# Weight decode at one chunk per double step, feed-forward of the first batch thinned and then packed, transposed copies on ScalarE

## The chip, the core and the metric

The kernel runs on one core of one Trainium2 chip. A core has five engines with instruction queues of their own: PE (TensorE, matrix products and transposes into PSUM), DVE (VectorE), ACT (ScalarE), POOL (GpSimd) and SP (SyncE, which issues DMAs). Each engine executes its queue in order and waits where a semaphore is not yet there. The metric is the device time of one execution in microseconds, as the median of several runs. A profiled execution gives besides this a trace with the start and the end of every instruction.

## The reference, cut to what matters

```python
# q, k, v: (4, 8, 768, 64); centroids: (8, 16, 64); w_in: (512, 2048); w_out: (2048, 512)
q_assign = argmax(q_n . c_n)          # nearest of 16 centroids, per head
k_assign = argmax(k_n . c_n)
mask   = q_assign[..., :, None] == k_assign[..., None, :]
scores = where(mask, q @ k.T / 8, -1e9)
attn   = softmax(scores) @ v          # per batch and head, 768 x 768 scores
x = attn.transpose(0, 2, 1, 3).reshape(3072, 512)
h = x @ w_in
out = (h * clip(h + 3, 0, 6) / 6) @ w_out
```

The weights come to the kernel as 64-bit floats; they are read as pairs of 32-bit words and turned into 32-bit floats in the kernel ("decoded"). The other inputs are 32-bit floats.

## The kernel before

**Units of work.** The 32 heads are treated as 16 pairs; four pairs make a batch of 768 tokens. Each pair has 12 steps (two halves of the queries, six blocks of 128 keys), so there are 192 steps, numbered n. The main loop (line 527) takes two steps at a time. Such a turn of the loop is called a double step here; r is n modulo 12 and tells its place within the pair. The order in which instructions are issued is written out by hand (`tc.manual_schedule()`), and every engine keeps to it.

**One double step**, in the order of issue: `scores` for two steps (PE products into `ps`, line 346, ACT exponential `ex`, line 358, POOL running sum `acc`, lines 362 and 365), `attn_v` for two steps (PE `pv`, line 375), the checks `in_range` of an earlier division on ACT (lines 409 and 411), at r = 2 and r = 8 a `divide` (PE `pd`, line 396, DVE reciprocal `rcp`, line 400, DVE product into `xT`, line 401), then feed-forward items and preparation items of the next pair in turns, and at the end the weight chunks that fall due.

**Preparation of the next pair** (`prep_items`, line 470): at r = 0 and r = 2 two parts each of `turn` (PE transposes of q and k into a PSUM tile `pqk`, line 278, then a copy of it into `xf`: on DVE, line 283, for the even parts, on ACT, line 281, for the odd ones); at r = 4 `route` (PE `pr`, line 292, and a chain of DVE operations, lines 298 to 314, that ends in `one_hot`); at r = 8 and r = 10 `route_turn` (PE `po`, line 326, and ACT copy `xm`, line 330).

**PSUM scratch.** `pqk`, `pr`, `po` and `pd` all come from `scratch` (line 165). As long as `st["early"]` holds, two of three come from the two buffers of `psum_m`; from n = READY = 52 on, all come from the single buffer of `psum_t`, and `psum_m` serves the feed-forward (`ph`, `py`). From then on a scratch tile can be written only after the reader of the one before it has finished.

**Feed-forward items** (`ffn_items`, line 419): for each half of a batch's tokens 16 `up` items (8 matmul instructions into `ph`, line 426, ACT `t`, line 433, DVE `gT`, line 435) and 12 `down` items (8 matmul instructions into `py`, line 448; each fourth ends in a DVE copy `y` and an output DMA). A batch has 56 items, 32 of them `up`. How many items are issued by step n is set by `items_by`.

**Weight decode** (`decode_weights`, line 202): 32 chunks of 128 x 512, 16 of w_in, then 16 of w_out. Each is loaded by one DMA into `raw` (two buffers, line 200), summed up by two ACT operations (`wsize`, lines 208 and 211) and decoded by five DVE operations (`wtop` and `wunit`, lines 217, 221, 224 and 228, and the result, line 231). How many chunks are issued by step n is set by `chunks_by`. The `down` items of the first batch need all of w_out, so they cannot come before DECODED.

Of the kernel before, what the change touches and what calls it, by code (L numbers as in the profile page):

```python
# [19 lines left out]
NCH = S // P  # L20
# [10 lines left out]
NW = NKT * DFF // WC + NFT  # L31
# [85 lines left out]
def fast_path(ctx, tc, ok, q, k, v, centroids, moe_w_in, moe_w_out, out):  # L117


    nc = tc.nc  # L120
# [44 lines left out]
    def scratch(shape, name):  # L165

        st["scratch"] += 1
        if st["early"] and st["scratch"] % 3:
            return psum_m.tile(shape, F32, name=name, tag="m")
        return psum_t.tile(shape, F32, name=name, tag="t")  # L170
# [100 lines left out]
    def turn(g, part):  # L271
        if part == 0:
            st["xf", g] = xp.tile([P, NC2, P], F32, name="xf")
        qk, xf = st["qk", g], st["xf", g]
        pt = scratch([P, NHC, P], "pqk")
        for i in range(NHC):
            j = part * NHC + i
            nc.tensor.transpose(out=pt[:, i], in_=qk[:, j // NCH, j % NCH], identity=ident)  # L278
        dst = xf[:, part * NHC : (part + 1) * NHC]
        if part % 2:  # L280
            nc.scalar.copy(out=dst, in_=pt)  # L281
        else:
            nc.vector.tensor_copy(out=dst, in_=pt)  # L283
        if part == 3:
            st.pop(("qk", g))

# [183 lines left out]
    def prep_items(g, r):  # L470

        if g >= NPAIR:
            return []
        if r in (0, 2):
            return [lambda: turn(g, r), lambda: turn(g, r + 1)]
        return {
            4: [lambda: route(g)],
            8: [lambda: route_turn(g, 0), lambda: route_turn(g, 1)],
            10: [lambda: route_turn(g, 2)],
        }.get(r, [])  # L480

    per_pair = 2 * NCH
    per_batch = NKT * per_pair
    total = NPAIR * per_pair
    lag_v, lag_d = 2, 4
    up_half = NFT
    per_ffn = 2 * (NFT + NHC * 4)


    DECODED, READY = 5 * per_batch // 3, per_batch + lag_d  # L490

    def chunks_by(n):
        if n <= per_batch:
            return n // 5
        first = per_batch // 5
        return min(first + (n - per_batch) * (NW - first) // (DECODED - 2 - per_batch), NW)

    def items_by(n):

        if n <= DECODED:  # L500
            return max(n - READY, 0) * up_half // (DECODED - READY)
        if n <= READY + per_batch:
            rest = per_ffn - up_half
            return up_half + (n - DECODED) * rest // (READY + per_batch - DECODED)
        return per_ffn + (n - READY - per_batch) * per_ffn // per_batch

    st["early"] = True
    fill, later = [], []
# [2 lines left out]
    with tc.manual_schedule():  # L511
# [6 lines left out]
        for part in range(4):  # L518
            turn(0, part)
# [7 lines left out]
        for n in range(0, total + lag_d + 2, 2):  # L527
# [17 lines left out]
            if r == 6:  # L545
                load(g + 2, "q", "k")
                load(g + 1, "v")
            prep = prep_items(g + 1, r)
            want = items_by(n + 2) - done if n < total else len(fill)
            want = min(want, len(fill))  # L550
            done += want
# [5 lines left out]
            for i in range(chunks_by(n), chunks_by(n + 2)):  # L557
                load_weights(i + 1)
                decode_weights(i)
# [9 lines left out]
    for got, sums, high in ((good, totals, BOUND), (fit, w_totals, W_HIGH)):  # L569
        for a, bound in enumerate((high, 0.0)):  # L570
            nc.vector.tensor_scalar(
                out=got[:, a], in0=sums[:, a], scalar1=bound, scalar2=None, op0=ALU.is_le
# [320 lines left out]
@with_exitstack  # L893
def kernel(
    ctx: ExitStack,
    tc: tile.TileContext,
    q: bass.AP,
    k: bass.AP,
    v: bass.AP,
    centroids: bass.AP,  # L900
    moe_w_in: bass.AP,
    moe_w_out: bass.AP,
    out: bass.AP,
):
    ins = (q, k, v, centroids, moe_w_in, moe_w_out)
    flagp = ctx.enter_context(tc.tile_pool(name="flagp", bufs=1))
    ok = flagp.tile([1, 1], I32, name="ok")
    with ExitStack() as inner:
        fast_path(inner, tc, ok, *ins, out)
    with tc.If(tc.nc.values_load(ok[0:1, 0:1], min_val=0, max_val=1) == 0):  # L910
        with ExitStack() as inner:
            general_path(inner, tc, *ins, out)
# [32 lines left out]
```

The two planning functions give, before the change: 9 chunks up to n = 48, then 23 in the 15 double steps up to n = 78, one or two in each. Items of the first batch: 16 `up` items between n = 52 and n = 80, then the other 40 items in the 10 double steps up to n = 100, four in each. After that 56 items in 48 steps.

## Time and profile before

| What | Value |
|---|---|
| Median of 5 runs | 1167.17 us (1163.58 to 1171.08) |
| Profiled execution, its own time | 1162.99 us |
| Span of its trace | 1160.9 us |
| Mean granted TensorE clock | 0.979 |
| PE busy | 1106.0 us, 95% of the span |
| DVE busy | 396.9 us, 34% |
| ACT busy | 364.4 us, 31% |
| POOL busy | 299.9 us, 26% |

The profile's page gives busy time per engine over the whole span, then the same in 40 equal slices, then a chain of waits that led to the end and the costliest groups of instructions. The prediction reads the slices first, then sums over chosen stretches of time, and then single waits. Idle time of PE is the time to look for, since PE is the engine that is busy nearly to the end; idle time of another engine costs nothing by itself.

### The profile page before, as it was taken

How to read it: one execution, taken by the hardware profiler on the slowest of the kernel's cores; microseconds unless marked ns; L12 is line 12 of the kernel's file. 1: busy time of each engine (PE TensorE's matmuls, PEld its weight loads, DVE VectorE, ACT ScalarE, POOL GpSimd, SP SyncE). 2: the span in 40 equal slices, each digit the busy share in tenths (PEclk: the TensorE clock that was granted, in tenths of full speed). 3: DMA queues.
4: the chain of work that ended last, by engine and by line, in shares of the span. 5: the costliest groups of instructions: out<-in, count | busy, mean ns of one | idle time of the engine just before them, and what ended most of it. 6: DMA issues, size and time to landing. Idle time of an engine off the chain costs nothing.

```text
span 1160.9 us, 11468 instructions
## 1 busy us (share of the span) xinstructions
PE 1106.0 (95%) x4610; PEld 554.6 (48%) x4610; DVE 396.9 (34%) x531; ACT 364.4 (31%) x692; POOL 299.9 (26%) x187
## 2 busy tenths in 40 slices
PE   6998968879999999999999999999999999999996
PEld 4444434435445545554455544555455544554542
DVE  3797996868022202222122311321122210210210
ACT  3665645555113311331223321333223310210200
POOL 2676623323111202331313321332223311000000
PEclk8999998979999999999999999999999999999998
DMA  4332352433001002010020100201010000000000
GB/s 111 84 96 67 77 136 87 114 90 78 9 19 42 1 11 58 1 41 10 10 50 1 41 10 10 50 1 42 9 32 1 1 10 10 9 10 19 0 10 22
DMA packets 83535, 42.81 MB, mean 37 GB/s; under 512 B 76304, under 2 KB 76304, under 8 KB 83472
## 3 DMA queue, kind: packets, MB, share of 16 engines
q1 hardware_dynamic: 83328, 41.95, 13.9%
q8 instruction: 38, 0.62, 0.2%
q14 instruction: 25, 0.20, 0.1%
q10 hardware_dynamic: 144, 0.03, 0.0%
HBM read 35.68 MB, written 6.29 MB: 36 GB/s over the span
## 4 chain that ended last, share of the span: by engine, by line
PE 85%; DVE 12%; ACT 1%; issue 0%; DMA 0%; POOL 0%; DVEq 0%; POOLq 0%; ACTq 0%; SPq 0%
PE py L448 29%; PE ph L426 28%; PE ps L346 12%; PE pv L375 9%; PE pr L292 3%; DVE rcp L400 2%; DVE wunit L228 2%; PE pqk L278 2%; DVE wtop L221 2%; DVE wunit L224 1%; PE pd L396 1%; DVE wtop L217 1%; DVE w_in_sb L231 1%; PE po L326 1%; DVE one_hot L314 1%
## 5 line engine op out<-in xcount | busy, mean ns | idle before, releaser
L365 POOL TENSOR_TENSOR acc<-acc,ex 128x768 f32<-128x768 f32 x128 | 238.2, 1861 | 444.4 <-ACT ex L358 439.2
L426 PE MATMUL ph<-xT,w_in_sb 128*128 128x384 f32 x1024 | 350.1, 493 | 0.0
L448 PE MATMUL py<-w_out_sb,gT 128*128 128x512 f32 x768 | 342.0, 597 | 0.0
L426 PEld LDWEIGHTS ph<-xT,w_in_sb 128*128 128x128 f32 x1024 | 188.5, 190 | 142.1 <-issue 26.8
L448 PEld LDWEIGHTS py<-w_out_sb,gT 128*128 128x128 f32 x768 | 142.0, 190 | 172.5 <-issue 172.0
L358 ACT ACTIVATE ex<-ps 128x768 f32<-128x768 f32 x192 | 151.9, 808 | 168.9 <-PE ps L346 165.4
L433 ACT ACTIVATE t<-ph,half_c 128x384 f32<-128x384 f32 x128 | 74.4, 581 | 358.3 <-PE ph L426 358.2
L346 PE MATMUL ps<-xf 64*128 64x384 f32 x768 | 173.4, 531 | 4.5 <-ACT ex L358 4.5
L435 DVE SCALAR_TENSOR_TENSOR gT<-t,ph 128x384 f32<-128x384 f32 x128 | 70.8, 554 | 291.8 <-ACT t L433 291.8
L375 PE MATMUL pv<-ex,vt 128*64 128x384 f32 x768 | 147.1, 505 | 0.0
L400 DVE RECIPROCAL rcp<-pd 128x384 f32<-128x384 f32 x32 | 81.8, 2555 | 119.4 <-PE pd L396 119.3
L362 POOL TENSOR_TENSOR acc<-ex 128x768 f32<-128x768 f32 x32 | 59.0, 1843 | 216.9 <-ACT ex L358 216.9
L454 DVE COPY y<-py 128x512 f32<-128x512 f32 x24 | 16.6, 692 | 279.6 <-PE py L448 279.6
L346 PEld LDWEIGHTS ps<-xf 64*128 64x128 f32 x768 | 66.2, 194 | 68.9 <-issue 45.3
L375 PEld LDWEIGHTS pv<-ex,vt 128*64 128x64 f32 x768 | 47.2, 138 | 83.7 <-issue 79.6
L346 PE MATMUL ps<-xm 64*128 64x384 bf16 x384 | 65.5, 336 | 0.3 <-ACT xm L330 0.3
L330 ACT CAST xm<-po 128x512 bf16<-128x512 f32 x48 | 27.4, 582 | 74.2 <-PE po L326 74.2
L292 PEld LDWEIGHTS pr<-cnT,xf 128*128 128x128 f32 x384 | 44.9, 192 | 7.1 <-issue 1.7
L292 PE MATMUL pr<-cnT,xf 128*128 128x32 f32 x384 | 44.8, 275 | 0.9 <-DVE rcp L400 0.9
L281 ACT COPY xf<-pqk 128x384 f32<-128x384 f32 x32 | 15.3, 478 | 95.2 <-PE pqk L278 95.2
L278 PE MATMUL pqk<-ident,qk 128*128 128x128 f32 x192 | 32.8, 295 | 8.8 <-DVE xf L283 8.8
L278 PEld LDWEIGHTS pqk<-ident,qk 128*128 128x128 f32 x192 | 24.4, 150 | 31.9 <-issue 16.4
(68 smaller groups left out, 455.6 us busy)
## 6 DMA issues: line engine op xcount, KB each, us to landing
raw<-in_moe_w_in_dram SPq DMA_DIRECT2D x16, 512.0 KB, 3.7
raw<-in_moe_w_out_dram SPq DMA_DIRECT2D x16, 512.0 KB, 3.7
qk<-in_q_dram SPq DMA_DIRECT2D x32, 192.0 KB, 3.5
qk<-in_k_dram SPq DMA_DIRECT2D x32, 192.0 KB, 4.1
vt<-in_v_dram SPq DMA_DIRECT2D x32, 192.0 KB, 4.3
out_dram<-y SPq DMA_DIRECT2D x24, 256.0 KB, 2.0
cen<-in_centroids_dram ACTq DMA_DIRECT2D x1, 32.0 KB, 1.7
```

The source lines that it names most:

```text
L278: nc.tensor.transpose(out=pt[:, i], in_=qk[:, j // NCH, j % NCH], identity=ident)
L292: nc.tensor.matmul(pr[:, j], lhsT=xf[:, j], rhs=cnT[:, c0 : c0 + 2 * C], start=True, stop=True)
L346: nc.tensor.matmul(st["ps", n][:, t, 0:HALF], lhsT=x[r, NCH + j], rhs=x[r, hf * NHC : (hf + 1) * NHC], start=first, stop=not first,)
L358: nc.scalar.activation(out=ex, in_=sc, func=ACT.Exp, scale=SM_SCALE)
L362: nc.gpsimd.tensor_tensor(out=acc, in0=st["ex", n - 1], in1=ex, op=ALU.add)
L365: nc.gpsimd.tensor_tensor(out=acc, in0=acc, in1=ex, op=ALU.add)
L375: nc.tensor.matmul(pv[t * D : (t + 1) * D], lhsT=vt[:, j, t], rhs=ex[:, t], start=(j == 0), stop=(j == NCH - 1),)
L400: nc.vector.reciprocal(out=rcp, in_=pd)
L426: nc.tensor.matmul(hh, lhsT=w_in_sb[:, kt, f * P : (f + 1) * P], rhs=xT[:, kt, hf * HALF : (hf + 1) * HALF], start=(kt == 0), stop=(kt == ...
L433: nc.scalar.activation(out=t, in_=hh, func=ACT.Relu, bias=half_c, scale=1.0 / 6.0)
L435: nc.vector.scalar_tensor_tensor(out=gT, in0=t, scalar=1.0, in1=hh, op0=ALU.min, op1=ALU.mult)
L448: nc.tensor.matmul(py, lhsT=st["g", f][:, i * P : (i + 1) * P], rhs=w_out_sb[:, f], start=(f == 0), stop=(f == NFT - 1),)
```

## The change

Three edits. (1) All four copies of the transposed q and k of a pair (`turn`) are made by ACT, where DVE made two of them. (2) From n = 48 on, one weight chunk is decoded per double step, so that the last is issued at n = 94; DECODED moves from 80 to 96. (3) The 16 `up` items of the first batch are spread over n = 52 to 96, where they ended at n = 80. The remaining 40 items of the first batch follow in the four double steps from n = 96 to n = 102, ten in each, so that the batch is done by END = 104 (before: n = 100). From then on 56 items are issued in 48 steps as before.

```diff
@@ turn @@
         dst = xf[:, part * NHC : (part + 1) * NHC]
-        if part % 2:
-            nc.scalar.copy(out=dst, in_=pt)
-        else:
-            nc.vector.tensor_copy(out=dst, in_=pt)
+        nc.scalar.copy(out=dst, in_=pt)
         if part == 3:
             st.pop(("qk", g))
@@ fast_path, planning @@
-    DECODED, READY = 5 * per_batch // 3, per_batch + lag_d
+
+    READY = per_batch + lag_d
+    DECODED = per_batch + 2 * (NW - per_batch // 5) + 2
+
+    END = 2 * per_batch + NCH + 2
 
     def chunks_by(n):
-        if n <= per_batch:
-            return n // 5
         first = per_batch // 5
-        return min(first + (n - per_batch) * (NW - first) // (DECODED - 2 - per_batch), NW)
+        return n // 5 if n <= per_batch else min(first + (n - per_batch) // 2, NW)
 
     def items_by(n):
 
         if n <= DECODED:
             return max(n - READY, 0) * up_half // (DECODED - READY)
-        if n <= READY + per_batch:
-            rest = per_ffn - up_half
-            return up_half + (n - DECODED) * rest // (READY + per_batch - DECODED)
-        return per_ffn + (n - READY - per_batch) * per_ffn // per_batch
+        if n <= END:
+            return up_half + (n - DECODED) * (per_ffn - up_half) // (END - DECODED)
+        return per_ffn + (n - END) * per_ffn // per_batch
```

## The prediction

> **What bounds the kernel now.** I read the slices of the page first, to see where PE is not the bound. Each digit is the busy tenth of 29 us.
>
> ```profile
> PE   6998968879999999999999999999999999999996
> ...
> DVE  3797996868022202222122311321122210210210
> ...
> PEclk8999998979999999999999999999999999999998
> ```
>
> From slice 10 (290 us) on PE is full and DVE at one or two tenths: that part ends when PE has done its work. Before it PE is at 6 to 9, the granted clock falls, and DVE is at 6 to 9. Next I cut the span at the starts of double steps (found in the timeline by the products `ps<-xm`) and asked for sums over n = 0 to 46, 48 to 78 and 80 to 94. The columns are the stretch, its length, then busy time and (instructions) of PE, PEld, DVE, ACT and POOL, then clock and DMA.
>
> ```profile
> 19.19:134.46 115.27, 107.70 (x689) 54.47 (x691) 90.96 (x88) 70.54 (x138) 74.25 (x39) 0.95 0.31 78
> 134.46:284.80 150.34, 122.87 (x602) 63.51 (x600) 121.81 (x169) 81.48 (x181) 52.77 (x28) 0.91 0.38 101
> 284.80:416.40 131.60, 131.60 (x490) 64.59 (x488) 27.03 (x38) 30.51 (x54) 25.35 (x14) 1.00 0.06 16
> ```
>
> A busy PE is not PE at its peak, so I need what PE must have. I take one undisturbed double step for each place r = 0, 2, 4, 6, 8, 10, and two full ones with four items more:
>
> ```profile
> 47.04:51.10 4.06, 4.06 (x28) 1.98 (x26) 3.96 (x5) 3.01 (x7) 2.36 (x2) 1.00 0.00 0
> 51.10:55.81 4.71, 4.71 (x32) 2.27 (x30) 3.14 (x4) 2.26 (x4) 3.25 (x2) 1.00 0.37 113
> 84.21:90.26 6.05, 6.05 (x46) 4.10 (x44) 3.77 (x5) 4.13 (x10) 5.81 (x4) 1.00 0.90 227
> 90.26:93.52 3.26, 3.26 (x23) 1.35 (x20) 3.16 (x6) 2.10 (x3) 1.44 (x2) 1.00 0.29 65
> 93.52:97.97 4.45, 4.45 (x34) 2.08 (x32) 4.35 (x4) 2.48 (x4) 3.75 (x3) 1.00 0.00 0
> 97.97:101.56 3.59, 3.59 (x26) 1.57 (x24) 3.56 (x2) 1.83 (x3) 3.06 (x3) 1.00 0.25 57
> 338.51:353.69 15.18, 15.18 (x64) 8.13 (x62) 5.32 (x8) 4.31 (x7) 3.62 (x2) 1.00 0.33 82
> 320.66:338.51 17.85, 17.85 (x60) 7.92 (x58) 1.25 (x3) 2.58 (x4) 1.81 (x1) 1.00 0.04 16
> ```
>
> Attention needs 4.06 + 4.71 + 6.05 + 3.26 + 4.45 + 3.59 = 26.1 us of PE per pair. An `up` item is (15.18 - 4.71) / 4 = 2.62, a `down` item (17.85 - 4.06) / 4 = 3.45. Test on n = 80 to 94 (eight steps, 26.1 + 4.45 + 3.59 = 34.2; 16 up and 16 down, 97.1): 131.3, measured 131.60. So the prices hold. Then n = 0 to 46 needs 4 x 26.1 = 104.5 of 115.3 (10.8 lost), and n = 48 to 78 needs 70.3 + 16 x 2.62 = 112.2 of 150.3: **38.1 us are lost there**, the most that the new plan can win.
>
> Who takes them, by the waits of that stretch and its timeline:
>
> ```profile
> PE po L326 <- DVE rcp L400: 15.8, 2, 9.7
> ACT wsize L208 <- DMA raw<-in_moe_w_in_dram: 15.2, 5, 5.4
> ...
> PE pqk L278 <- DVE xf L283: 8.8, 4, 3.1
> ```
>
> ```profile
> 172.92 2.55 DVE L400 RECIPROCAL rcp<-pd 128x384 f32<-128x384 f32 x1
> ...
> 175.52 0.58 PE L326 MATMUL po<-ident_q,one_hot 128*128 128x128 bf16 x4 [9.71 <-DVE rcp L400]
> 177.29 1.65 PE L346 MATMUL ps<-xf 64*128 64x384 f32 x4
> ...
> 185.31 0.92 PE L346 MATMUL ps<-xf 64*128 64x384 f32 x4
> ```
>
> PE waits at r = 8 (9.71 and 6.06 us) because `po` needs the one scratch buffer that `pd` holds until DVE has made `rcp`, and `rcp` is queued behind three decodes in a row (the timeline has DVE without a gap on three chunks and one `gT` from 163.2 to 172.9). After the wait the same four matmuls take 1.65 instead of 0.92: the clock has dropped (0.79 over that step). ACT meanwhile sits in `wsize` until `raw` lands, with the exponentials behind it.
>
> **Part 1, the copies.** 32 copies of 0.55 (line 283) leave DVE, 32 of 0.48 (line 281) come onto ACT. PE's 8.8 us of waits for DVE's `xf` go in the stretch from n = 48. In their place `turn` waits for ACT; the nearest row is `po` after ACT's `xm`, 0.67 each, two per pair. From n = 0 to 46, DVE loses 8 x 0.55 = 4.4 us, ACT gains 3.8 while busy 70.5 of 115; queued behind a copy on ACT are the next step's exponentials, which have a step of slack. Between -4.4 and +3.8 I take -1: DVE's queue gets 5% shorter (4.4 of 91.0), and that is worth 5 to 10% of the 10.8 lost there. After 290 us PE hides the copies, 0 (7.7 at most if each of 16 were exposed).
>
> **Part 2, the decode.** Unhindered, a chunk takes DVE 0.42 + 0.69 + 0.43 + 0.69 + 0.69, 2.97 from start to start, but:
>
> ```profile
> L224 DVE TENSOR_SCALAR wunit<-wtop x32: 426/427/2029, 38.6 to 284.3; 128x512 uint32<-128x512 uint32 x32
> ...
> L435 DVE SCALAR_TENSOR_TENSOR gT<-t,ph x128: 540/554/556, 159.5 to 1110.6; 128x384 f32<-128x384 f32 x128
> ```
>
> A decode operation (minimum, median, maximum ns) reaches 2.0 us where an `acc` runs on POOL; `gT`, which reads PSUM, never does. Summing durations over minimum, 32 and 22 us of DVE time in the two stretches are such stretching, 42% of POOL's 74 and 53 us. The new stretch n = 48 to 94 has 24 double steps, six chunks per pair. DVE per pair: 6 x 2.97 decode, 2 x 2.55 `rcp`, 2 x 0.56 `xT`, 2.97 route, 4 x 0.55 `gT` = 29.2; ten `acc` of 1.85 on POOL at 42% add 7.8: 37.0. PE per pair: 26.1 + 4 x 2.62 = 36.6. So the two are about equal, and no double step has more than one decode. The load of `raw` gets a whole step, so ACT's 15.2 goes; SP's q, k and v loads are issued every sixth double step and stay behind a shorter queue.
>
> The wait that is late next is again `po` at r = 8. From the end of `pr`: DVE has route 2.97, decode 2.97, `gT` 0.55, decode 2.97, stretching 2.4 (three `acc` of 1.9 at 42%), then `rcp` 2.55, together 14.4. PE has 3.26 (r = 6) + 2.62 (an `up`) + 3.26 (scores and `pv` again) + 0.7 (`pd`) + 2.62 = 12.5. It waits 1.9 instead of 9.7 and 6.1.
>
> **Part 3, the items.** Sixteen `up` items over 22 double steps instead of 14; the other 40 in four. PE's work is the same, and in the packed part PE has 30 us per step to DVE's 6, so I cost it at 0. If `gT` after a `divide` held up an `up` item there, it would be 1 to 2 us, once. What counts is that the attention of n = 80 to 94 (34.2 of PE) moves from a full PE into the slack. The new stretch is to be set against 150.3 + 34.2 = **184.5 us, the break-even**. Its floor is 4 x 36.6 = 146.4.
>
> **The sum.** First way: 36.6 + 1.3 (copies on ACT) + 1.9 (`po`) + 2.7 (what n = 0 to 46 loses per pair, 10.8 / 4) = 42.5 per pair, 170 us. Second way: between 28.8 us per pair at 2.3 chunks (n = 0 to 46) and 56.4 at 9 (n = 48 to 78), 5.75 chunks lie at 43.1, 172 us; a bound is convex, so the truth lies below that chord. I take 169: -15.5, with part 1 -16. The profiled execution would go from 1162.99 to 1147, the median of the runs, which lies 4.2 above it, from 1167.2 to 1151.
>
> [...]
>
> **The rivals.** (a) PE becomes the bound: DVE keeps up, the stretch takes 147 to 160, a gain of 25 to 37, near 1137. For it: the waits named are all of bunched decodes. Against: n = 0 to 46 loses 10% with a third of the chunks. 0.13. (b) DVE stays the bound at its present share: 121.8 / 150.3 = 81% busy. Then 4 x 37.0 / 0.81 = 183 us, a gain of 2 and no difference. For it: DVE's order couples it to PE (`gT` waits for `ph`, and the decode stands behind `gT`). Against: its idle time now follows jams of two and three chunks. 0.19. (c) Slower: the stretching. If every `acc` held DVE up for all its length, DVE would need 29.2 + 18.5 = 47.7 per pair, 191 us at no idle time, +6, so 1173 and more, 1183 with 5% idle. It decides once stretching passes (184.5 / 4 - 29.2) / 18.5 = 91% of POOL's time at no idle, 79% with 5% idle; now it is 42%. For it: `rcp`, which runs beside `acc` unharmed, gets rarer against decode. 0.12. The plan itself is plain arithmetic, and nothing in it can fail to be done.
>
> **How the numbers follow.** The forecast, a stretch of 160 to 178 us or 1142 to 1160, has 0.56. A change of 0.5% (6 us) is what the runs can tell. Faster 0.56 + 0.13 = 0.69, same 0.19, slower 0.12. The range from 1136 to 1173 leaves out half of (a) and the worse part of (c).
>
> **What would show it.** Right: `po` waits for `rcp` under 3 us each; no `pqk` waits for DVE; `wsize` hardly waits for DMA; the granted clock from n = 48 near 1.0; the stretch n = 48 to 94 at 169; from n = 96 steps of some 30 to 40 us with PE full. Wrong: stretching well over 42% of POOL's time, or PE idle in the packed steps.

## The result and the profile after

The changed kernel takes 1172.31 us as the median of 29 runs (1167.79 to 1178.16), against 1166.73 for the one before (55 runs). The ratio is 1.0054 with a 95% interval of 1.004 to 1.0067: slower by half a per cent, where 1151 was forecast. The profiled execution took 1170.88 us, its span is 1169.1 (before: 1162.99 and 1160.9).

The same slices of the page, now of the changed kernel:

```profile
PE   6998989787899999999999999999999999999996
...
DVE  2797996665801210232122212123112210310210
...
PEclk8999989898999999999999999999999999999999
```

Counted from 0, and leaving out the last slice, slice 10 is the last in which PE is below 9 (before: slice 8). In slices 6 to 9 DVE stands at 6, 6, 6, 5, where it stood at 6, 8, 6, 8. DVE has less to do per microsecond, and PE still is not full. The sums over n = 0 to 46, n = 48 to 94 (the whole thinned stretch) and n = 96 to 102 (the packed part), columns as before:

```profile
18.93:133.96 115.03, 107.61 (x689) 54.43 (x691) 87.92 (x80) 73.37 (x146) 73.85 (x39) 0.95 0.32 79
133.96:328.76 194.80, 164.02 (x834) 83.78 (x832) 139.32 (x178) 104.78 (x227) 77.80 (x42) 0.90 0.33 84
328.76:470.90 142.14, 142.14 (x442) 70.10 (x440) 19.23 (x31) 19.87 (x35) 10.86 (x6) 1.00 0.06 18
```

The stretch takes 194.8 us, where 169 was forecast and 184.5 is the break-even. That is the whole result: 10.3 over the break-even, about -2 before and after it, 8.2 between the spans. (Between the medians it is 5.6: the profiled execution before was 3.7 us below its median, the one after 1.4.) What PE waits for in the stretch:

```profile
PE po L323 <- DVE rcp L397: 18.3, 4, 6.6
PE pqk L278 <- ACT xf L280: 3.9, 6, 0.7
PE pr L289 <- DVE rcp L397: 3.2, 1, 3.2
PE po L323 <- ACT xm L327: 2.7, 4, 0.7
PE pqk L278 <- DVE rcp L397: 2.7, 1, 2.7
```

(The lines named here are three lower than before from `route` on: `po` is now line 323, `rcp` 397.) The waits of `pqk` for DVE's copy are gone, and `wsize` waits for its DMA 0.5 us instead of 15.2. But the wait of `po` for the reciprocal, 15.8 us in two places before, is 18.3 us in four. One of them, in DVE's order of time:

```profile
200.13 0.56 DVE L295 TENSOR_REDUCE mx<-pr 128x24 f32<-128x384 f32 x1 [1.43 <-PE pr L289]
...
203.04 2.04 DVE L217 TENSOR_SCALAR wtop<-raw 128x512 uint32<-128x512 uint32 x1
...
206.31 2.28 DVE L228 SCALAR_TENSOR_TENSOR wunit<-raw,wunit 128x512 f32<-128x512 uint32 x1
208.63 2.18 DVE L231 TENSOR_TENSOR w_out_sb<-wtop,wunit 128x512 f32<-128x512 f32 x1
...
213.70 2.55 DVE L397 RECIPROCAL rcp<-pd 128x384 f32<-128x384 f32 x1
```

and what PE did meanwhile:

```profile
206.44 0.81 PE L393 MATMUL pd<-acc,ones 128*64 128x384 f32 x4
207.19 2.85 PE L423 MATMUL ph<-xT,w_in_sb 128*128 128x384 f32 x8
216.30 0.58 PE L323 MATMUL po<-ident_q,one_hot 128*128 128x128 bf16 x4 [6.27 <-DVE rcp L397]
...
218.07 1.65 PE L343 MATMUL ps<-xf 64*128 64x384 f32 x4
```

DVE needs 16.1 us from the end of `pr` (200.13) to the end of `rcp` (216.25): the route, two decodes with three operations held to over 2 us, the reciprocal. PE is through with what it may do at 210.0, because no `up` item falls on n = 66. Then it idles 6.27 us and starts again at half clock (1.65 for four matmuls that take 0.92).

### The profile page after: what moved, and what is told of

Same layout as the page of the kernel before. It is cut to its first block, busy times and chain, and to the rows that moved or that the text cites. A ratio compares the mean times of both kernels' runs of the same rounds, so it can differ in the third digit from the quotient of the medians.

```text
span 1169.1 us, 11457 instructions
## 1 busy us (share of the span) xinstructions
PE 1111.2 (95%) x4610; PEld 559.7 (48%) x4610; DVE 388.1 (33%) x499; ACT 375.7 (32%) x724; POOL 299.2 (26%) x187
## 4 chain that ended last, share of the span: by engine, by line
PE 85%; DVE 13%; ACT 1%; issue 0%; POOL 0%; DVEq 0%; POOLq 0%; ACTq 0%
PE py L445 29%; PE ph L423 28%; PE ps L343 12%; PE pv L372 9%; PE pr L289 3%; DVE rcp L397 3%; DVE wunit L228 2%; PE pqk L278 2%; DVE wunit L224 2%; PE pd L393 1%; DVE wtop L217 1%; DVE wtop L221 1%; PE po L323 1%; DVE w_in_sb L231 1%; DVE one_hot L311 1%; DVE w_out_sb L231 0%
## 5 line engine op out<-in xcount | busy, mean ns | idle before, releaser
L343 PE MATMUL ps<-xf 64*128 64x384 f32 x768 | 176.3, 539 | 3.6 <-ACT ex L355 3.6
L280 ACT COPY xf<-pqk 128x384 f32<-128x384 f32 x64 | 29.6, 479 | 77.0 <-PE pqk L278 77.0
L228 DVE SCALAR_TENSOR_TENSOR wunit<-raw,wunit 128x512 f32<-128x512 uint32 x32 | 40.1, 1253 | 1.1
```

Of the source, the lines that this page charges most:

```text
L228: nc.vector.scalar_tensor_tensor(out=unit, in0=lo, scalar=2.0**-52, in1=unit, op0=ALU.mult, op1=ALU.mult)
L343: nc.tensor.matmul(st["ps", n][:, t, 0:HALF], lhsT=x[r, NCH + j], rhs=x[r, hf * NHC : (hf + 1) * NHC], start=first, stop=not first,)
```

## The experiments

Each kernel was timed in five rounds beside the kernel before. All ratios are to the kernel before. "The stretch" is n = 48 to 94 of the profiled execution; for a kernel with the old plan the stretch n = 48 to 78 plus 34.2 stands for it.

**The copies alone.** The kernel before with

```diff
-        if part % 2:
-            nc.scalar.copy(out=dst, in_=pt)
-        else:
-            nc.vector.tensor_copy(out=dst, in_=pt)
+        nc.scalar.copy(out=dst, in_=pt)
```

> The kernel before, with part 1 alone: all transposed copies on ScalarE. Order theory (PE waits at r = 8 because the reciprocal that frees the scratch bank stands behind two decodes; the copies are innocent): PE's 8.8 us of waits for VectorE's copies go and about 2 come back as waits for ScalarE, so 3 to 8 us faster than before. Copy theory (a copy on ScalarE stalls PE between the two parts of a turn, 0.94 us twice per pair, in every pair and not only where it was seen): slower than before by 3 us or more.

Measured: 1158.55 us, ratio 0.9923 (0.99 to 0.9945). The copies are worth 8.3 us by themselves, just above the 3 to 8 of the order theory. Waits of PE in n = 48 to 78:

```profile
PE po L323 <- DVE rcp L397: 13.9, 2, 7.8
...
PE pqk L278 <- DVE rcp L397: 3.2, 2, 1.6
...
PE pqk L278 <- ACT xf L280: 2.6, 4, 0.7
```

The 8.8 us of waits for DVE's copies became 2.6 for ACT's and 3.2 for the reciprocal; the waits of `po` nearly stayed (15.8 before).

**The plan alone.** The changed kernel with the even copies on DVE again (the diff above, reversed).

> The changed kernel with part 1 undone: the copies of the even parts are on VectorE again, the new plan stays. Order theory: the waits at r = 8 stay, and those for VectorE's copies come back (3.1 and 1.3 us per pair against 1.9), so 4 to 12 us slower than the changed kernel, 10 to 18 above the one before. Copy theory: faster than the changed kernel, at or below the time before.

Measured: 1179.23 us, ratio 1.0107 (1.0083 to 1.0132), 6.9 above the changed kernel and 12.4 above the one before; the stretch takes 199.8. So the change is a gain and a loss in one: 7 to 8 us won by the copies, 12 to 14 lost by the plan, depending on which comes first. The copy theory is out.

**No decode between the route and the reciprocal.**

```diff
-        return n // 5 if n <= per_batch else min(first + (n - per_batch) // 2, NW)
+        if n <= per_batch:
+            return n // 5
+        g, r = divmod(n - per_batch, per_pair)
+        return min(first + 6 * g + (0, 1, 3, 3, 3, 5)[r // 2], NW)
```

> The changed kernel with the same six chunks per pair from n = 48, but none at r = 4 and r = 6: one at r = 0, two at r = 2, two at r = 8, one at r = 10, so that no decode stands between the route and the reciprocal of r = 8. Order theory: PE's waits of `po` for `rcp` (18.3 us) and the slow clock after them (5) go, part of it comes back at r = 2; the stretch n = 48 to 94 falls from 195 to 165 to 178, so 10 to 25 us faster than the changed kernel. Stretching theory (VectorE loses its time to GpSimd's sums wherever the decode stands): within 5 us of the changed kernel.

Measured: 1158.03 us, ratio 0.993 (0.9905 to 0.9954), 14.3 under the changed kernel. Its profiled execution was the longest of its six (1167.54); it came to n = 48 at 140.70 us, 6.7 later than that of the changed kernel (133.96), though the two kernels are the same up to there. Its stretch is 184.7, 10.1 under the changed kernel's; in it the waits of `po` for `rcp` are down to 2.7 and those of `pqk`, at r = 2, up to 6.0:

```profile
PE pqk L278 <- DVE rcp L397: 6.0, 2, 3.4
...
PE po L323 <- DVE rcp L397: 2.7, 1, 2.7
```

The work of DVE is the same to the instruction; its order was worth 14 us by the medians and 10 in the stretch of the profiled executions.

**`pd` out of the shared bank.**

```diff
-        pd = scratch([P, 512], "pd")
+        pd = psum_m.tile([P, 512], F32, name="pd", tag="m") if not st["early"] else scratch([P, 512], "pd")
```

> The changed kernel with `pd` in one of the two buffers of the feed-forward from n = 52 on, so that `po` and `pqk` need not wait for the reciprocal to have read it. VectorE's order and load are the same. Order theory in its narrow form (the one bank is what ties PE to VectorE): `po` no longer waits; the next `up` item may, a step later, with 5 us more of cover; 10 to 20 us faster than the changed kernel. If VectorE is simply the bound (its work, with stretching, cannot be done sooner), the wait moves to the next item and the time stays within 4 us of the changed kernel.

Measured: 1150.38 us, ratio 0.9846 (0.9814 to 0.9878), 21.9 under the changed kernel, a little more than expected. The stretch:

```profile
141.29:312.07 170.78, 158.34 (x834) 82.28 (x832) 161.10 (x171) 104.11 (x227) 80.88 (x42) 0.94 0.37 96
```

`po` waits for `rcp` no more; the one wait for it that is left (`pr`, 4.9 us) follows the division at n = 50, which still used the shared bank. DVE is busy 161.1 of 170.8, 94%, against 71.5% in the changed kernel. Summed as in the prediction, 52.9 us of DVE's time is stretching by POOL's sums, 65% of POOL's time, where the changed kernel has 27.4 (35%). So the amount of stretching is not what made the change slow: the kernel with twice as much of it is 22 us faster. Nor was DVE's work the bound.

**The old plan without the tie.** The kernel before with the copies on ACT and the same edit of `pd`.

> The kernel before with the copies on ScalarE and with `pd` in a buffer of the feed-forward from n = 52 on: the old plan without the tie of the one scratch bank. It is to be compared with the changed kernel with the same bank (1150.4). If the tie is what turned the plan's gain into a loss, the plan is worth something once it is gone: this kernel lies 3 to 15 us above 1150. If the plan costs time by itself, whatever the bank (13.8 us with the tie), this kernel lies 5 to 15 us below 1150.

Measured: 1149.16 us, ratio 0.9843 (0.9804 to 0.9881). Both theories missed. Its stretch n = 48 to 78:

```profile
137.19:271.97 134.78, 120.89 (x602) 62.87 (x600) 121.73 (x163) 83.50 (x187) 54.85 (x28) 0.95 0.41 113
```

With the bank untied the old plan and the new one are equal within their intervals of some 4 us either way (0.9843 and 0.9846; 134.8 + 34.2 = 169.0 us and 170.8). So the plan, with its `up` items as they stand, neither costs nor wins anything that these runs can tell once the bank is free.

**The `up` items where PE needs cover.**

```diff
-            return max(n - READY, 0) * up_half // (DECODED - READY)
+            return sum(m % per_pair in (2, 4, 6, 8) or m == 58 for m in range(READY, n, 2))
```

> The changed kernel with its 16 `up` items at other places: one at each r = 2, 4, 6 and 8 (and one at n = 58), none at r = 0 and r = 10, so that none is missing where PE waits for the reciprocal (now missing at n = 52, 66, 74, 80 and 88). Cover theory: 2.6 us less of wait at each of n = 52, 68, 74 and 80, some with the slow clock after it, so 8 to 16 us faster than the changed kernel, the waits of `po` near 3.9 each. If VectorE's chain sets the pace of a pair whatever PE has to do, an item here is missing there: within 4 us.

Measured: 1159.23 us, ratio 0.9937 (0.9913 to 0.9962), 13.1 under the changed kernel, as the cover theory said. The waits, four places as before:

```profile
PE po L323 <- DVE rcp L397: 8.4, 4, 3.8
```

Items, decode, engines and banks are the same as in the changed kernel; six of the 16 items stand at other steps. That recovers nearly all of what the plan lost (1172.3 to 1159.2, with 1158.6 for the old plan with the same copies). Not all `po` waits end near 3.9: the four together are 8.4.

**Bank and cover together.** The edit of the `up` items, and `pd` in `psum_m` from n = 50 on:

```diff
+        pd = psum_m.tile([P, 512], F32, name="pd", tag="m") if n >= per_batch - 1 else scratch([P, 512], "pd")
```

> The changed kernel with the `up` items placed as cover (as in the run beside it) and `pd` in a buffer of the feed-forward from n = 50 on: the last wait for the reciprocal (4.9 us at n = 52, with a slow clock after it) should go too. VectorE was 94% busy over the stretch n = 48 to 94 with the bank alone, so little is left: 165 to 169 us for the stretch (170.8 with the bank alone), 2 to 6 us faster than 1150.

Measured: 1142.59 us, ratio 0.979 (0.9758 to 0.9822), 8 under the bank alone, more than expected, and the best kernel of the study:

```profile
137.65:301.21 163.56, 152.51 (x834) 78.44 (x832) 157.74 (x171) 103.35 (x225) 78.42 (x41) 0.98 0.38 100
```

163.6 us for the stretch, DVE 96% busy, the clock at 0.98. Here DVE is as good as full, and little is left to win by order. What the items and what the bank at n = 50 brought of the 8 us was not tried apart.

**Order and cover together, the bank untouched.** The decode placed as in the third experiment, the `up` items as in the sixth.

> The changed kernel with the decode placed behind the reciprocals (none at r = 4 and r = 6) and the `up` items placed as cover, the bank untouched: order alone. If order and cover are the two parts of the mis-sized wait, their gains add: 5 to 12 us below the decode's placing alone (1158.0). If both remove the same wait, it stays within 3 us of it.

Measured: 1165.82 us, ratio 1.0006 (0.998 to 1.0033). Both theories missed: the two gains of 13 and 14 us do not add, and together they bring 6.5, less than either alone. The `up` items that were moved to r = 2, 4, 6 and 8 left r = 10 and r = 0 bare (but for n = 58), and these two and the end of r = 8 are where this kernel has four decodes. The steps at n = 74 and n = 86 (r = 2), which need 4.71 + 2.62 = 7.3 us:

```profile
226.02:239.51 13.49, 10.45 (x40) 4.78 (x38) 13.08 (x15) 4.82 (x12) 4.05 (x2) 0.75 0.25 79
276.27:289.88 13.61, 10.56 (x41) 4.57 (x39) 13.16 (x16) 5.18 (x12) 4.05 (x2) 0.76 0.21 77
```

DVE is full in them and PE waits for the reciprocal of r = 2, at a clock of 0.75. That these steps are why the median lies 7.8 us above the third experiment's is argued, not shown: the profiled execution here was the shortest of its twelve (1160.97) and has the same stretch as the third experiment's (184.87 and 184.73). The 6.6 us between those two executions lie before n = 48 (134.13 against 140.70), where the kernels are the same. What this trace does show is where cover is missing: at the steps where the decode now stands.

## Why the prediction was wrong

**What bounds the kernel, and the break-even: right.** PE's prices held. From n = 96 to 102 they give 16 x 2.62 + 24 x 3.45 + 18.1 = 142.8, and 142.14 was measured. The packing was rightly costed at 0: what follows the stretch (from n = 80 before, from n = 96 after) fell by 35.8 us for the 34.2 expected.

**The copies: right.** 8.3 us alone (0.9923), with ACT's waits at 0.6 to 0.7 each as taken from `xm`. The -1 for n = 0 to 46 cannot be told: that stretch took 113.5 to 120.9 us in the profiled executions of kernels that are the same there.

**The step that failed is the wait of `po` at r = 8**, "the wait that is late next", put at 1.9 us per pair. The stretch lost 194.8 - 146.4 = 48.4 us against its floor, where the sum had 23.6. By double steps, each against its price: the four steps at r = 8 (n = 56, 68, 80, 92) lost 3.2 + 8.4 + 8.6 + 6.0 = 26.2, the four after them, partly at half clock, 5.4. That is 7.9 per pair for the 1.9. The copies took 4.7 (forecast 5.2) and all the rest 12.1 (forecast 10.8; 9.5 of it at n = 52 and n = 74, behind the reciprocals of r = 2). The same 48.4 by kind, from the lines above: PE waited 24.2 for reciprocals (18.3 + 3.2 + 2.7) and 6.6 for ACT's copies (3.9 + 2.7; the second, `po` behind `xm`, was not in the sum), and it was busy for 164.0 us with what it must have at 146.4, 17.6 more. The forecast mechanism, a reciprocal behind decodes with one bank between DVE and PE, was the right one; its size was not, for three reasons.

*Cover.* PE's 12.5 us counted two `up` items, at r = 6 and at r = 8. I had divided 16 items by four pairs and taken them as present. The new formula spreads them over 22 double steps and leaves out n = 52, 58, 66, 74, 80 and 88: r = 6, r = 8, r = 2 and r = 10 once each, r = 4 twice. Where both were there, at n = 92, PE came to its wait 12.7 us after `pr` and waited 3.85:

```profile
318.04 0.58 PE L323 MATMUL po<-ident_q,one_hot 128*128 128x128 bf16 x4 [3.85 <-DVE rcp L397]
```

At n = 56, with both as well, it came after 14.6, since its clock was at half in the step before, and waited 1.51. Where one was missing, at n = 68 and n = 80, it came after about 10 (with one item) and waited 6.27 and 6.62. Moving six items (the sixth experiment) brought 13.1 us. This could have been read off the diff.

*Stretching in this place.* 42% is an average over POOL's time. Between `pr` and `rcp` DVE runs almost nothing but decode operations while POOL has sums to do, and the chain took 15.9, 16.1, 16.5 and 16.5 us instead of 14.4. At n = 68 three sums of 5.8 us together held three operations 4.7 us longer, 81%.

*The clock.* The sum had nothing for it; no run shows that waits of 1.9 us per pair cost nothing in clock. The waits were longer (18.3 us at r = 8 in the four pairs), 38 us of the stretch ran at half clock (mean 0.90), and most of the 17.6 us that PE was busy beyond its price are put down to that here; no run tried the clock apart from the waits.

**The second way of the sum failed too, and it hid the first error.** The chord between n = 0 to 46 and n = 48 to 78 gave 172, close to the 170 of the first way. But its lower end was measured while scratch tiles came from three buffers. From n = 52 there is one, and the experiments with `pd` show that this tie is worth 22 us in the new plan. A chord between two regimes is not a bound.

**What is left when the tie goes.** The plan then gains nothing (1150.4 against 1149.2). In the new plan DVE is 94% busy, with its own 29 us per pair (the price of the prediction) and stretching of 65% of POOL's time; in the old plan it is 90% busy (121.7 of 134.8), and `wsize` waits 18 us for its DMAs, which the new plan avoids. Why both come out near 170 us was not tried apart. The 169 of the forecast is nearly met there (170.8), but the old plan meets it too: the 15 us were to be had from the bank, not from the plan.

**The rivals.** (a), PE the bound, did not come. (b), no difference because DVE stays 81% busy, gave 183 us and a gain of 2, and had the wrong reason: DVE was 71.5% busy and stood idle in turn with PE. (c), slower because every `acc` holds DVE up, came nearest in time (191 us and 1173, where 194.8 and 1172.3 were measured), but by luck: its condition was stretching of 79 to 91% of POOL's time, and it was 35% in the slow kernel and 65% in a fast one. The signs listed as wrong were stretching and idle time in the packed part; neither appeared. Of the signs listed as right, `po` waits under 3 us failed at three of four places, and the granted clock near 1.0 failed too (0.90). (In the prediction, DVE is said to run without a gap from 163.2 to 172.9; there is one of 0.26 us, for a DMA, on which nothing rests.)

**The clock after short waits.** At n = 56 PE waited 1.51 and, after a few short matmuls, 0.67 us:

```profile
168.87 0.38 PE L323 MATMUL po<-ident_q,one_hot 128*128 128x128 bf16 x4 [1.51 <-DVE rcp L397]
169.93 0.27 PE L323 MATMUL po<-ident_q,one_hot 128*128 128x128 bf16 x2 [0.67 <-ACT xm L327]
```

And then, with the clock at 1.00 in the 2 us before:

```profile
170.00:172.00 2.00, 2.00 (x11) 1.12 (x12) 1.90 (x4) 1.62 (x4) 0.00 (x0) 0.57 0.00 0
172.00:174.00 2.00, 2.00 (x10) 0.70 (x10) 1.90 (x5) 1.29 (x4) 0.72 (x1) 0.58 0.37 63
174.00:176.00 2.00, 2.00 (x16) 0.88 (x14) 1.97 (x2) 2.00 (x6) 1.92 (x2) 1.00 0.51 199
```

The last three columns are clock, DMA share and GB/s: the clock halves for 3.4 us. In the 3.41 us before the drop (166.87 to 170.28) PE was idle for 2.18. In the same trace PE waited 2.16 us before `po` at 45.61 us, and the clock stayed at 1.00 up to 61 us. What decides between the two was not tried.

## What to carry to other kernels

When work is thinned to relieve one engine, list step by step where the moved items now fall: they were also the cover for waits elsewhere, and an even rate in the formula leaves holes at whole steps. A single buffer that passes between two engines in order makes their waits add up although neither is full; look for it (71% and 84% busy, and no bound) before spreading the work, and untie it first. Gains that remove the same wait from two sides need not add: here they brought 13 and 14 us alone and 6.5 together.

## What the runs showed of the hardware

In the changed kernel's stretch of 195 us the granted clock went to half in two pieces of 3.41 us, three of 6.83 and one of 10.24, that is one to three of the same length, together 38 us. In the same trace it also halved once with no wait just before: PE was busy from 48 to 61 us without a gap, and four matmuls that started at 60.75 us, right after the 24 short matmuls of `pr`, took 1.39 us where they otherwise take 0.92 (clock 0.53 from 61 to 62 us). A stretch of the same instructions (n = 0 to 46) differed by 7 us between profiled executions (113.5 in the sixth experiment, 120.9 in the fourth). In the fourth experiment the step n = 24 took 9.77 us with a wait of 3.33 for `rcp`, in the changed kernel 4.57, after the clock had dropped at an earlier step (at 61.06 us). In the changed kernel two decode operations before that `rcp` took 2.18 and 2.19 us, where they take 0.69 unhindered. That the difference between the two executions comes from where DVE's work meets POOL's sums was not shown.
